# Redrawing the issue order, PSUM banks and exp buffers of a linear-attention + MLP-Mixer kernel

## The chip, the cores and the metric

The kernel runs on one core of a Trainium2 chip. The metric is device microseconds of one execution; the number given is the median of several timed runs. Beside the timed runs stands one execution taken with the hardware profiler, whose trace all views come from.

## What is computed

Linear attention with the ELU+1 feature map over 8 batches, 8 heads, 576 positions and 64 columns a head, then an MLP-Mixer over the 576 x 512 result of each batch: token mixing (576 to 256 and back), and channel mixing (512 to 1536 and back), each with its residual.

```python
def phi(x):
    return np.where(x > 0, x, np.exp(x) - 1.0) + 1.0
q_p, k_p = (phi(q), phi(k))
kv = np.einsum('bhsd,bhse->bhde', k_p, v)
z = np.sum(k_p, axis=2)
num = np.einsum('bhsd,bhde->bhse', q_p, kv)
den = np.einsum('bhsd,bhd->bhs', q_p, z)[..., None] + 1e-06
x = num / den                       # heads side by side: 576 x 512 a batch
...
h = np.maximum(xt @ w_tok1, 0.0) @ w_tok2          # xt: x transposed
u = x + h.transpose(0, 2, 1)
h2 = np.maximum(u @ w_ch1, 0.0) @ w_ch2
return (u + h2).astype(np.float32)
```

## The kernel before

The kernel is a list of 1114 named steps. Each name stands for one short function that issues a handful of instructions on one engine, and a loop at the end (line 1026) walks the string `ORDER` (line 62) and issues the steps as they stand. Every engine and every DMA queue works through its own instructions in that order; waits between engines follow from the data, on whole regions of a buffer: a step waits for every earlier step in the list that touches the same region. Four tables name places: `BANK` the PSUM bank of each accumulator (8 banks), `EBUF` which of three buffers an exponential goes to, `YBUF` and `SLOT` others. All the data of a batch passes through the steps in a pipeline several batches deep, so that at any time four or so batches are in work.

A name begins with its batch (0 to 7; 8 is the set of the last 64 positions of all batches together). Where a step has two halves, a last digit 0 or 1 names it.

- `nLq`, `nLk`, `nLv` (line 223): loads of q, k and v, on SP's queue. `nqT` (330), `nuT` (484) and `nut` (489): DMA transposes of the features of q, of u, and of the tail rows of u, on the same queue.
- `nqx`, `nkx` (ScalarE, 247) the exponential; `nqa`, `nka` (VectorE, 251) max(x + 1, 1); `nqb`, `nkb` (VectorE, 257) the smaller of both. `nv` (270) the cast of v, on ScalarE with two exceptions.
- `nK` (TensorE, 297) the products of k and v of a batch, `nKc` (ScalarE, 303) their two copies out of PSUM; `nn` (TensorE, 383) q times them; `nd` (ScalarE, 393) the denominators, `nnd` (VectorE, 398) the reciprocal, `nn0` to `nn2` and `nnt` (VectorE, 402) and `no` (ScalarE, 423) the scaled results. Batch 1 transposes its q on TensorE (`1Q`, 315) and not by DMA.
- Token mixing: `nf` (TensorE, 450), `nfr` (ScalarE, 455); `ng` (TensorE, 462), `ngu` (VectorE, 468) which adds the residual; `ngt` and `ngv` (475, 479) the same for tail rows of two batches.
- Channel mixing, both products in Strassen-Winograd's form with seven products of blocks. Batch 0 is done plainly (`0m`, `1m` for the first product of batches 0 and 1, line 653, read by `0r`, `1r`, line 660 and 662; `0q`, 674). For the others: `ns1` to `ns4` (VectorE, 790) the sums of blocks of the transposed u; `nxgi` (TensorE, 828) product i of column group g, read by `nygi` (VectorE 648, ScalarE 841 and 843); `nw` (VectorE, 752) sums of blocks of the hidden layer; `npij` (TensorE, 870) product i, half j, of the second product; `nc` (ScalarE, 911) and `neZ`, `neW`, `neY`, `neX` (VectorE, 917) read them, and `nhZ`, `nhW`, `nhY` (GpSimd, 924) add three parts into the output buffer. `ws` (GpSimd, 725) and `G` (VectorE, 802) are sums of weight blocks.
- Output: `noa`, `nob` (GpSimd's queue, 928), `0o0`, `0o1` (685), and for the tails `8R` (VectorE, 883) and `8D` (889).

`nhZ` and `nhY` follow `neZ` and `neY`, `nhW` follows `neW`; X and W share the odd row pairs of the buffer, Z and Y the even ones, and an `nh` waits for whichever `ne` of its rows stands before it in the list.

```python
def pair_more(n, z, i):
    d, c = PAIR[z]
    o = slots(f"{n}P", 4)[:, d::2, HC[c]]
    nc.gpsimd.tensor_tensor(out=o, in0=o, in1=part[i], op=ALU.add)
...
def u_sums(n, which):
    t = tuc
    b11, b12, b21, b22 = [ublock(n, h, e) for h in range(2) for e in range(2)]
    x_, y_ = {1: (b12, b11), 2: (b22, t[0]), 3: (b22, b12), 4: (b21, t[1])}[which]
    (nc.gpsimd if f"{n}s{which}" in ON_POOL else nc.vector).tensor_tensor(
        out=t[which - 1], in0=x_, in1=y_, op=ALU.subtract)
```

Of the kernel before, what the change touches and what calls it, by code (L numbers as in the profile page):

```python
# [41 lines left out]
BANK = {k_: int(v_) for k_, v_ in (e.split(":") for e in """2K:2 2n0:6 2n1:2 2n2:0 2f:5 2g0:4 2g1:1 2X2:4 2Z2:2 2Y2:6 3K:4 3n0:6 3n1:0 3n2:4 3f:0 3g0:0 3g1:0 3X2:6 3Z2:5 3Y2:5  # L42
3gt:7 4K:2 4n0:2 4n1:0 4n2:4 4f:0 4g0:0 4g1:0 4X2:3 4Z2:0 4Y2:2 5K:0 5n0:3 5n1:6 5n2:0 5f:6 5g0:6 5g1:6 5X2:2 5Z2:1
5Y2:0 5gt:5 6K:2 6n0:6 6n1:0 6n2:2 6f:6 6g0:6 6g1:4 6X2:5 6Z2:7 6Y2:4 7K:4 7n0:6 7n1:2 7n2:4 7f:6 7g0:6 7g1:6 7X2:7
7Z2:0 7Y2:3 7gt:0 1h00:1 1h01:3 1h10:2 1h11:4 1t0:5 1t1:1 1t2:3 1t3:0 1m0:4 1m1:2 1m2:5 1m3:1 1m4:3 1m5:6 1m6:0 1m7:5
1m8:1 1m9:5 1m10:4 1m11:5 7X0:0 7Z0:3 7Y0:4 7X1:5 7Z1:6 7Y1:1 1PX:2 1PZ:0 1PY:7 2PX:7 2PZ:6 2PY:6 3PX:2 3PZ:5 3PY:5
4PX:4 4PZ:4 4PY:5 5PX:1 5PZ:2 5PY:0 6PX:2 6PZ:5 6PY:6 warm0:0 0Q00:1 0Q01:2 0s0:3 warm1:0 0Q10:1 0Q11:2 warm2:3 0K0:4
0d0:0 0n0:6 0l0:1 0s1:2 0K1:4 0d1:3 0n1:6 0l1:0 0f0:1 0f1:4 0g00:2 0g01:3 0g10:0 0t0:6 0t1:4 0g11:1 0m0:6 0m1:5 0t2:7
0t3:4 0m2:3 0m3:7 0m4:0 0m5:2 0m6:7 0m7:4 0m8:6 0m9:2 0m10:1 0m11:3 U00:0 U01:5 1Q0:1 U02:6 U03:7 1Q1:1 1K:3 1n00:1
1n01:1 1n10:3 1n11:3 1n20:3 1n21:1 1f:3 2X1:5 2Z1:4 2Y1:7 3X1:3 3Z1:4 3Y1:4 4X1:4 4Z1:1 4Y1:1 5X1:3 5Z1:5 5Y1:7 6X1:3  # L50
6Z1:1 6Y1:6 2X0:3 2Z0:6 2Y0:2 3X0:2 3Z0:4 3Y0:7 4X0:0 4Z0:1 4Y0:5 5X0:6 5Z0:0 5Y0:5 6X0:2 6Z0:0 6Y0:1 1gt:0 7PX:0
7PY:4 7PZ:1 8X0:4 8X1:6 8X2:7 8Y0:2 8Y1:3 8Y2:5 8Z0:1 8Z1:4 8Z2:5 8PX0:7 8PX1:2 8PY0:6 8PY1:3 8PZ0:1 8PZ1:5""".split())}
# [57 lines left out]
def kernel(  # L110
# [134 lines left out]
    def phi_exp(nm, n, c):  # L245
        f = raw[nm, rb(n)][:, 2 * c:2 * c + 2].rearrange("p j f -> p (j f)")
        nc.scalar.activation(out=ebuf[EBUF[f"{n}{nm}{c}"]], in_=f, func=AF.Exp)  # L247

# [808 lines left out]
```

## Time and profile before

| what | value |
|---|---|
| timed runs, us | 249.76, 249.89, 250.34; median 249.89 |
| profiled execution, us | 250.8 |
| its span, first to last instruction, us | 249.0 |
| granted TensorE clock, mean | 0.993 |
| instructions in the trace | 6343 |

The page of the profile gives for each engine the time in which it was busy, its share of the span and its number of instructions; PE is TensorE's matmuls, PEld its weight loads, DVE is VectorE, ACT ScalarE, POOL GpSimd and SP the engine that issues loads and transposes. A list by stretches of time gives the same between two cuts. In a timeline a line has its start, its duration, the engine, the line of code, the operation and its tiles, and in square brackets how long the engine had stood idle and which instruction released it.

### The profile page before, as it was taken

How to read it: one execution, taken by the hardware profiler on the slowest of the kernel's cores; microseconds unless marked ns; L12 is line 12 of the kernel's file. 1: busy time of each engine (PE TensorE's matmuls, PEld its weight loads, DVE VectorE, ACT ScalarE, POOL GpSimd, SP SyncE). 2: the span in 40 equal slices, each digit the busy share in tenths (PEclk: the TensorE clock that was granted, in tenths of full speed). 3: DMA queues.
4: the chain of work that ended last, by engine and by line, in shares of the span. 5: the costliest groups of instructions: out<-in, count | busy, mean ns of one | idle time of the engine just before them, and what ended most of it. 6: DMA issues, size and time to landing. Idle time of an engine off the chain costs nothing.

```text
span 249.0 us, 6343 instructions
## 1 busy us (share of the span) xinstructions
PE 232.2 (93%) x2556; PEld 174.1 (70%) x2570; DVE 218.0 (88%) x374; ACT 147.1 (59%) x268; POOL 81.6 (33%) x93
## 2 busy tenths in 40 slices
...
GB/s 241 263 203 259 343 218 259 406 317 340 307 139 280 371 198 178 364 210 203 194 315 277 69 159 212 327 84 153 113 3 179 99 0 4 5 166 0 8 151 180
DMA packets 50349, 48.55 MB, mean 195 GB/s; under 512 B 30736, under 2 KB 36240, under 8 KB 50320
## 3 DMA queue, kind: packets, MB, share of 16 engines
...
## 4 chain that ended last, share of the span: by engine, by line
PE 71%; DMA 15%; DVE 5%; POOL 3%; issue 2%; ACT 1%; SPq 1%; DVEq 0%; POOLq 0%; ACTq 0%
PE ps L870 26%; PE ps L828 23%; PE ps L450 6%; DMA uT<-u 6%; DMA q_raw<-in_q_dram 5%; DMA wc<-in_moe_w_ch_dram 4%; PE ps L674 4%; PE ps L462 4%; PE ps L653 3%; PE ps L297 2%; PE ps L383 1%; DVE sums L790 1%; POOL qT L966 1%; DVE obuf L917 1%; PE ps L514 1%
## 5 line engine op out<-in xcount | busy, mean ns | idle before, releaser
L828 PEld LDWEIGHTS <-swc 128*128 128x128 bf16 x336 | 32.7, 98 | 7.6 <-DVE sums L790 1.1
L828 PE MATMUL ps<-sums,swc 128*128 128x256 bf16 x252 | 34.4, 273 | 1.2 <-DVE sums L790 1.2
L870 PEld LDWEIGHTS <-cr 128*128 128x128 bf16 x288 | 27.9, 98 | 4.3 <-issue 0.3
L870 PE MATMUL ps<-k_raw,v_raw 128*128 128x256 bf16 x252 | 30.8, 273 | 0.1
L924 POOL TENSOR_TENSOR obuf<-obuf,q_raw 128x512 f32<-128x512 f32 x7 | 9.7, 1381 | 63.5 <-ACT q_raw L911 26.1
L828 PEld LDWEIGHTS <-wc 128*128 128x128 bf16 x252 | 24.5, 98 | 5.0 <-issue 0.8
L843 ACT COPY v_raw<-ps 128x512 f32<-128x512 f32 x35 | 20.3, 593 | 12.1 <-PE ps L828 7.1
L870 PEld LDWEIGHTS <-v_raw 128*128 128x128 bf16 x252 | 24.3, 98 | 3.6 <-issue 0.3
L648 DVE CUSTOM_DVE_ANT_0 cr<-ps,v_raw 128x512 bf16<-128x512 f32 x35 | 23.6, 682 | 2.2 <-PE ps L828 2.1
L928 POOL DMA_DIRECT2D out_dram<-obuf x28 | 17.7, 637 | 23.3 <-DVE obuf L917 16.9
L870 PE MATMUL ps<-wc,cr 128*128 128x256 bf16 x192 | 23.9, 273 | 0.0
L247 ACT ACTIVATE e<-q_raw 128x1152 bf16<-128x1152 f32 x16 | 18.7, 1170 | 8.2 <-DMA q_raw<-in_q_dram 8.0
L917 DVE TENSOR_TENSOR obuf<-ps,u 128x512 f32<-128x512 f32 x28 | 19.2, 686 | 4.7 <-PE ps L870 2.3
L653 PE MATMUL ps<-uT,wc 128*128 128x512 bf16 x92 | 21.5, 379 | 1.6 <-DVE xt L402 1.2
L247 ACT ACTIVATE e<-k_raw 128x1152 bf16<-128x1152 f32 x16 | 18.7, 1174 | 5.6 <-DMA k_raw<-in_k_dram 5.5
L828 PE MATMUL ps<-uT,wc 128*128 128x256 bf16 x144 | 20.6, 272 | 0.3
L841 ACT ACTIVATE cr<-ps 128x512 bf16<-128x512 f32 x21 | 12.0, 599 | 11.1 <-PE ps L828 10.4
L924 POOL TENSOR_TENSOR obuf<-obuf,part 128x512 f32<-128x512 f32 x7 | 9.8, 1406 | 24.5 <-DVE obuf L917 24.4
L653 PEld LDWEIGHTS <-wc 128*128 128x128 bf16 x96 | 9.1, 98 | 11.7 <-issue 1.7
L468 DVE TENSOR_TENSOR u<-ps,x 128x1024 bf16<-128x1024 f32 x12 | 14.6, 1218 | 1.5 <-PE ps L462 1.4
L752 DVE TENSOR_TENSOR v_raw<-cr 128x1536 bf16<-128x1536 bf16 (+3 forms) x21 | 14.1, 683 | 1.6 <-ACT cr L841 1.6
L924 POOL TENSOR_TENSOR obuf<-obuf,w 128x512 f32<-128x512 f32 x7 | 9.0, 1284 | 19.4 <-DVE obuf L917 19.2
...
## 6 DMA issues: line engine op xcount, KB each, us to landing
...
```

The lines of the kernel that those rows point to most:

```text
L247: nc.scalar.activation(out=ebuf[EBUF[f"{n}{nm}{c}"]], in_=f, func=AF.Exp)
L450: nc.tensor.matmul(out=banks(f"{n}f")[:, mt], lhsT=w1t[:, b, ms] if r == R else w1[:, r, ms], rhs=xt[n // 2 % 2] if r == R else x[b][:, r, :],
L468: nc.vector.tensor_tensor(out=u[b][:, rs], in0=banks(f"{n}g{i}"), in1=x[b][:, rs], op=ALU.add)
L648: nc.vector._custom_dve(TENSOR_ADD_SAT, out=o, in0=ps, in1=c, s0=3.4028234663852886e38, s1=0.0)
L653: nc.tensor.matmul(out=bank(f"{n}m{mc}"), lhsT=wc1[:, kj, 128 * mc:128 * mc + 128], rhs=uTj[b][:, kj] if n < 2 - U1 else uT[b][:, :, kj], ...
L752: return engine.tensor_tensor(out=s_[which - 1][:, ks], in0=x_, in1=y_, op=op)
L828: nc.tensor.matmul(out=ps[:, j], lhsT=lhs[:, k_, 128 * j:128 * (j + 1)], rhs=rhs[:, :, k_], start=(first and j == 0 and k_ == 0), stop=(k_ ...
L843: nc.scalar.copy(out={1: c1, 6: c6, 5: c5}[i], in_=ps)
L870: nc.tensor.matmul(out=ps, lhsT=lhs[:, k_], rhs=rhs[:, k_], start=(first and not skip and k_ == 0), stop=(k_ == KH - 1), skip_group_check= ...
L917: nc.vector.tensor_tensor(out=slots(f"{n}P", 4)[:, d::2, HC[c]], in0=pair_tile(n, "X" if z == "W" else z), in1=u[n % 2][:, d::2, HC[c]], o ...
L924: nc.gpsimd.tensor_tensor(out=o, in0=o, in1=part[i], op=ALU.add)
L928: nc.gpsimd.dma_start(out=outv[n, :, 2 * d + e:2 * d + e + 5:4], in_=slots(f"{n}P", 4)[half[e], d::2])
```

## The change

The change replaces three of the tables: `ORDER`, `BANK` and `EBUF`. `ORDER` holds the same 1114 names before and after, in another sequence; the first 56 (to `0mb1`) keep their places. Which engine does a step, the functions behind the names, the loads, buffers and their sizes stay. The sequence of transposes and loads on SP's queue is changed in the middle, and so are the positions of VectorE's steps against the sums on GpSimd. Of the diff, the lines named in the prediction (old ones first):

```diff
--- before.py
+++ after.py
@@ -39,71 +39,71 @@
...
-BANK = {k_: int(v_) for k_, v_ in (e.split(":") for e in """2K:2 2n0:6 2n1:2 2n2:0 2f:5 2g0:4 2g1:1 2X2:4 2Z2:2 2Y2:6 3K:4 3n0:6 3n1:0 3n2:4 3f:0 3g0:0 3g1:0 3X2:6 3Z2:5 3Y2:5
...
+BANK = {k_: int(v_) for k_, v_ in (e.split(":") for e in """2K:2 2n0:2 2n1:0 2n2:4 2f:5 2g0:0 2g1:6 2X2:3 2Z2:0 2Y2:0 3K:2 3n0:2 3n1:6 3n2:0 3f:6 3g0:6 3g1:6 3X2:1 3Z2:3 3Y2:2
...
 
-EBUF = {k_: int(v_) for k_, v_ in (e.split(":") for e in """0k0:0 0q0:1 0q1:2 0k1:0 1k0:1 1k1:0 1q0:0 1q1:1 2q0:2 2q1:1 2k0:0 2k1:2 3q0:1 3q1:0 3k0:1 3k1:2 4q1:2 4q0:2 4k0:1
-4k1:2 5k0:1 5k1:2 5q0:1 5q1:0 6k1:0 6k0:2 6q1:1 6q0:0 7k1:2 7k0:1 7q0:0 7q1:0""".split())}
+EBUF = {k_: int(v_) for k_, v_ in (e.split(":") for e in """0k0:0 0q0:1 0q1:2 0k1:0 1k0:2 1k1:2 1q0:0 1q1:1 2q0:0 2q1:2 2k0:1 2k1:0 3q0:2 3q1:1 3k0:0 3k1:0 4q1:1 4q0:1 4k0:0
+4k1:0 5k0:1 5k1:0 5q0:2 5q1:2 6k1:2 6k0:2 6q1:1 6q0:0 7k1:1 7k0:2 7q0:1 7q1:1""".split())}
 
...
 ORDER = """A2 A0 A1 A3 A4 A5 A6 A8 A9 A7 A10 A12 A13 A14 A11 A16 A17 A15 A19 A18 A21 A20 A22 A23 A24 A25 A26 A27 A28 A29 A30 A33
...
-0ma5 0mb5 0mb3 0ma2 B0 B1 G03 0mb2 0r5 1ka0 G02 G04 1kb0 0ma4 0mb4 0r2 0r4 0mb0 0r0 G21 G11 0r3 G12 0ma10 G22 0mb10
-G14 1kx1 0ma7 0r1 1ka1 0ma9 0mb9 1kb1 B2 2Lq0 0r10 0ma8 0mb8 0r8 0ma6 0mb6 0ma11 G13 0mb7 0r9 0r6 0q0 0mb11 1qx0 1qa0
...
-3qx1 1ma2 1mb2 1r5 2Kc0 2Kc1 1r2 ws20 ws30 1r8 1gv 2n 3qa0 1mb10 2d1 2d0 0o1 2d2 1r10 1ma11 1mb11 1r11 1ma0 1mb0 3qb0
-2nd 2o0 3qa1 2n2 1ma7 2nt 3kx0 1mb7 2o1 1r7 1ma6 1mb6 2n0 1ma3 1mb3 1r6 0o0 2n1 2f0 3qb1 3ka0 2f1 1r0 1r3 1w10 1w13
...
-3y16 2eW 5qa1 5Lv0 2eY 2p41 3y12 5v0 4n1 3x21 2p40 2hW 5Lv1 2eX 3y25 3y21 2hY 5qb1 5qa0 3x02 5qx0 4f1 3s3 4fr1 4f0
-3x26 3x05 4fr0 4g1 3y26 3y02 3y05 5qb0 5ka1 3x15 4gu1 3x23 3y23 3x03 3y06 3x07 2oa 6Lq1 6qx1 2ob 3x17 3y15 5v1 3x27
-4g0 3s4 3y07 3x04 3y27 3x22 3x13 3y17 4gu0 3ut 3y04 5kb1 3x24 3y24 3y22 3x14 3y14 5K 3y13 5Kc1 3p10 3p20 5qT1 3y03
-3w12 6Lv0 5qT0 3p21 3w10 6v0 3p11 3eZ 5Kc0 5n 3w22 5d1 3p50 3p51 5d0 3w20 5d2 3w30 3c0 3w40 5nd 5n2 6Lk1 5n0 3p61 3p60
-3hZ 3c2 3p31 3p30 4uT0 3c1 5o1 3p71 3p70 6ka1 5o0 4x21 6kx1 3eY 6Lk0 6kx0 4uT1 4x11 4s1 4x05 3hY 3oa 4y11 5nt 4x01 3eW
-3hW 6kb1 4y21 3p40 4x12 6Lq0 4s2 4y01 4x06 6ka0 5n1 4y12 6kb0 4x26 6Lv1 3p41 6v1 3eX 6qa0 4s3 6qx0 6qb0 5f0 4x16 6qa1
...
-6y07 7gv 7uT0 6x27 6y16 6x15 6x23 6y27 6y15 6x22 6x17 6y22 6x03 6x24 6y24 6y23 6x04 6x13 7x01 6y04 7x21 6y17 6x14 6y14
...
+0ma8 0ma4 0ma6 1kx0 0mb6 G01 G02 G04 1ka0 1kb0 B0 B1 B2 0ma5 0mb5 G21 G23 0r1 0r0 0r6 2Lq0 2Lq1 2Lv0 G03 0ma11 1kx1
+0mb8 0r8 0mb2 0r2 0mb11 1ka1 1kb1 0r11 G13 0mb4 0r5 0ma7 0mb7 0r4 0ma9 0mb9 G22 0r7 G11 1qx0 0ma10 1qx1 0mb10 G12 0r9
...
+2kx1 1r1 1ma8 1mb8 3qx0 1mb10 2v1 1ma9 2kb0 2ka1 1r8 2kb1 3qx1 1mb4 1r4 1mb5 1r5 0z2 1ma2 1mb2 0z3 1mb9 1r2 1r9 1gt
+1gv 1r10 ws10 2K ws20 1ma3 1mb3 2Kc0 2Kc1 2qT1 3qa0 2qT0 3qb0 2n 1r3 1ma7 1mb7 2d1 3qa1 1ma11 3Lk0 2d0 2d2 2nd 1mb11
+ws32 2n2 2nt 1r7 2n0 2n1 0o1 3Lv1 2o1 2o0 0o0 1r11 1w13 3Lk1 1ma0 1mb0 1r0 ws30 1ma6 1mb6 3qb1 1r6 1w10 2f0 2f1 3ka0
...
+2w30 2w40 3x12 5kx0 5kb0 4n2 2p71 2p70 2c2 2p31 2p30 3x01 5Lk1 5qa1 1ob 3x21 2eW 3y01 2p41 2p40 3y11 2eY 4n1 3y12 2eX
+2hZ 4f1 3s3 2hW 5qb1 5Lv1 4f0 5v1 3y21 6Lk0 3x22 4fr1 3x02 4fr0 4g0 3s1 3x25 5qa0 5qx0 3s2 3y02 4gu0 3x26 3x06 3x15
+5kx1 3y06 4g1 3x16 2hY 5qb0 3y22 3x05 3s4 3y26 3x27 2oa 4gu1 6Lq1 3x07 3y15 3x13 3y25 3y16 5Lv0 3y05 3y27 2ob 3y07
+3x17 3x03 6qx1 5ka1 3y17 3x04 5v0 5kb1 3x24 3y24 3x23 3y23 3x14 3y03 3y04 3y13 6Lv1 3y14 5K 3w10 6v1 5Kc1 3p20 5qT1
+3p10 3p11 5Kc0 3w12 3w20 3w22 5qT0 3c0 5n 5d0 3p21 3w30 4uT1 5d2 3eZ 3p61 5d1 5nd 5o0 5n0 5nt 3p60 3c1 3p50 3p51 3w40
+3c2 3hZ 4uT0 4x02 6Lk1 6ka1 6kx1 3p70 4x12 3p30 5n2 6kb1 4s1 3p31 6kx0 3eY 3hY 3oa 3p71 4x11 3eW 4x21 5n1 4x01 6ka0
+4y11 4s2 3p40 5o1 4y01 3p41 6Lv0 4y02 5f0 6Lq0 6qx0 5f1 4x16 4y12 5fr0 4y21 4x26 3eX 5fr1 5g1 4y16 4x15 4x25 7Lv1 4x06
+4y15 4x05 6kb0 6qa1 7Lq1 4s4 4s3 6qb1 3hW 3ob 4x13 6qa0 4y25 4x23 5gu1 4y26 4x27 4y05 6qb0 4x03 4y27 4y06 4x07 4y07
...
+5p60 4oa 5eZ 7ka1 5c1 5p50 7kb1 7K 7Kc1 5p51 5c2 6gu0 6uT0 5w30 6gu1 6uT1 5p70 5p71 7Kc0 7n 7d0 5w40 5p31 5p30 7d1 5eW
+7d2 5p40 5p41 7nd 7n2 7n1 7o0 7o1 5hW 6x11 6x01 7n0 7nt 5eY 5eX 7f0 7f1 6s1 6s2 6x21 5hZ 7fr0 6y01 6x02 6y11 6s3 7fr1
+6y02 6x12 6y12 6x15 7g0 6x06 6y06 6x05 6y21 6x22 7gu0 6y15 6x16 6y22 6s4 7g1 7gu1 6y05 6x13 6y16 6y13 6x26 6x07 6y07
+6x17 6y17 5hY 6y26 6x03 6x27 6y03 5oa 6x25 6y25 6x04 6x14 6y04 3ut 7gt 6w10 6w20 8x01 7gv 6x23 6y27 6y23 6w30 6p10
+7uT0 7x12 6x24 6y14 6y24 6w12 6w22 6w40 6p11 6c0 6p20 6p21 6p50 6p60 6p61 6c1 6p51 6c2 7x01 6p70 7uT1 7x11 7s1 5ob 7s2
+7s4 7y01 7x06 7x02 7y02 6p71 7y06 7s3 6p31 7y11 6eZ 6hZ 7x15 7y12 7y15 6p30 6eY 7x07 8y01 7x05 7y05 7ut 6hY 7y07 7x21
...
+8R20 8p51 8R51 8w44 7p41 7eX 8w32 8p60 8R60 8p61 8p50 8D210 8R50 8p70 8R70 8p31 8D211 8R61 8R31 8p30 8p71 7hZ 8p40
+8D311 8D310 8R30 8D200 8D201 8R71 8D710 7hY 7oa 8R40 8D711 8D700 8p41 8D701 8R41 8D410 7ob 8D411"""
```

76 lines of the change are left out of this document (33 added, 43 removed).

## The prediction

> **What bounds the kernel now.** I read the busy times first, then their split over seven stretches, cut where the waits of TensorE fall. Columns of a stretch: us from the start, length, busy time (instructions) of PE, PEld, DVE, ACT, POOL, granted clock, DMA share, GB/s.
>
> ```profile
> PE 232.2 (93%) x2556; PEld 174.1 (70%) x2570; DVE 218.0 (88%) x374; ACT 147.1 (59%) x268; POOL 81.6 (33%) x93
> 0.00:34.61 34.61, 29.54 (x264) 16.96 (x267) 26.13 (x56) 20.61 (x40) 16.41 (x28) 1.00 1.06 263
> 34.61:60.11 25.50, 24.92 (x299) 14.28 (x304) 23.96 (x48) 17.15 (x25) 13.98 (x12) 1.00 1.08 305
> 60.11:66.96 6.85, 5.58 (x62) 2.83 (x63) 6.76 (x9) 5.35 (x14) 5.14 (x6) 1.00 0.98 343
> 66.96:122.00 55.04, 54.62 (x700) 42.39 (x702) 53.93 (x85) 41.78 (x73) 13.30 (x14) 1.00 0.90 240
> 122.00:138.00 16.00, 12.94 (x144) 10.63 (x143) 13.91 (x21) 11.23 (x21) 5.47 (x5) 1.00 0.86 261
> 138.00:242.81 104.81, 104.57 (x1093) 86.96 (x1095) 92.84 (x160) 51.00 (x98) 27.29 (x30) 1.00 0.45 103
> 242.81:249.03 6.22, 0.00 (x0) 0.00 (x0) 0.42 (x1) 0.00 (x0) 0.00 (x0) 0.73 0.62 181
> ```
>
> TensorE sets the time, with VectorE close behind: in 66.96 to 122 TensorE idles 0.42 us in 55, VectorE 1.11. So another order can win only what TensorE idles (5.07 before 34.61; 0.58 + 1.27 + 0.42 + 3.06 + 0.24 = 5.57 behind it; 6.22 of final reads and stores), and it loses wherever VectorE, with a few per cent to spare, comes late. The largest piece is 122 to 138. The list of TensorE's waits (total, times, longest) and the timeline (start, duration, engine, operation, count, idle before and its releaser) tell what it is:
>
> ```profile
> PE ps L383 <- ACT kvbd L303: 1.5, 1, 1.5
> PE ps L828 <- DVE sums L790: 1.2, 2, 0.8
> PE ps L653 <- DVE xt L402: 1.2, 1, 1.2
> ...
> 123.50 1.16 ACT L270 CAST vs<-v_raw 128x1152 bf16<-128x1152 f32 x1 [2.23 <-DMA v_raw<-in_v_dram]
> 124.18 7.17 DMA uT<-u
> 124.67 0.38 ACT L303 CAST kvbd<-ps 64x260 bf16<-64x260 f32 x1
> 125.09 0.79 PE L383 MATMUL ps<-kvbd,qT 64*128 64x65 bf16 x40 [1.53 <-ACT kvbd L303]
> 130.90 1.27 POOL L924 TENSOR_TENSOR obuf<-obuf,w 128x512 f32<-128x512 f32 x1 [2.74 <-DVE obuf L917]
> 131.45 1.00 DVE L790 TENSOR_TENSOR sums<-uT 128x512 bf16<-128x512 bf16 x1 [0.70 <-DMA uT<-u]
> 132.50 0.60 PE L828 MATMUL ps<-sums,swc 128*128 128x256 bf16 x4 [0.39 <-DVE sums L790]
> 133.98 1.71 POOL L924 TENSOR_TENSOR obuf<-obuf,part 128x512 f32<-128x512 f32 x1 [0.29 <-DVE obuf L917]
> 134.47 1.50 DVE L790 TENSOR_TENSOR sums<-uT,sums 128x512 bf16<-128x512 bf16 x1
> 136.03 1.05 PE L828 MATMUL ps<-sums,swc 128*128 128x256 bf16 x8 [0.83 <-DVE sums L790]
> ```
>
> ScalarE waits 2.23 us in `6v0` for the load of v, so `5Kc0` behind it is late and `5n` stalls 1.53. Then `4uT1` (the second row of that time, from the chain) lands 7.17 us after its issue, `4s1` and `4s2` wait for it, and each runs long beside a GpSimd sum: 1.00 and 1.50.
>
> ```profile
> L790 DVE TENSOR_TENSOR sums<-uT,sums x6: 414/418/1499, 79.4 to 202.0; 128x512 bf16<-128x512 bf16 x6
> L924 POOL TENSOR_TENSOR obuf<-obuf,part x7: 1264/1285/1711, 80.6 to 238.9; 128x512 f32<-128x512 f32 x7
> L648 DVE CUSTOM_DVE_ANT_0 cr<-ps,v_raw x35: 675/681/693, 83.9 to 227.7; 128x512 bf16<-128x512 f32 x35
> 106.01 0.42 DVE L790 TENSOR_TENSOR sums<-uT,sums 128x512 bf16<-128x512 bf16 x1
> 106.35 0.68 DVE L917 TENSOR_TENSOR obuf<-ps,u 128x512 f32<-128x512 f32 x1
> 106.95 0.75 DVE L251 TENSOR_SCALAR y<-q_raw 128x1152 bf16<-128x1152 f32 x1
> 107.62 0.68 DVE L917 TENSOR_TENSOR obuf<-ps,u 128x512 f32<-128x512 f32 x1
> 107.17 1.66 POOL L924 TENSOR_TENSOR obuf<-obuf,part 128x512 f32<-128x512 f32 x1 [4.97 <-DVE obuf L917]
> ```
>
> The same sum on VectorE takes 414 ns alone (min/median/max of a line) and 1499 beside a GpSimd sum; the GpSimd sum takes 1264 alone and 1711 or 1.66 when an L251 was already running. A read out of PSUM never grows (675 to 693). So the two engines exclude each other where VectorE has SBUF alone as input (L251, L257, L752, L790): the one that comes second waits. The starts also give VectorE's slots: 0.34 for L790, 0.60 for L917 (L648 alike, 0.09 under its 0.68), 0.67 for L251 and L257.
>
> **The change part by part.** The same 1114 steps stand in both lists and each engine runs the same instructions; only orders, banks and E buffers differ. So nothing is costed by the number of instructions, and each place by what TensorE waits there. The slots of TensorE: eight 256-wide matmuls in 1.05 with the last 0.27 (row at 136.03), so 0.11 each; and from the next fence eight 512-wide ones in 1.89 with the last about 0.38, so 0.217.
>
> *Loads and transposes of batches 4 to 6 (122 to 138).* On SP's queue `5qT1 5qT0 4uT1 4uT0` now stand together, behind `6Lv1` and ahead of `6Lk1 6Lv0`; before, loads stood between all four. `6Lv0` moves behind the transposes, and `6v1` takes the place of `6v0` on ScalarE. A pair of transposes without loads between is in the trace:
>
> ```profile
> 72.09 3.03 SPq L484 DMA_TRANSPOSE uT<-u  x2
> ...
> L468 DVE TENSOR_TENSOR u<-ps,x x12: 1210/1218/1225, 70.8 to 191.3; 128x1024 bf16<-128x1024 f32 x12
> ```
>
> Both issued in 3.03 us there, against one that lands after 7.17 here. TensorE's work between `4g0` and the first `4x` that needs the transposes also grows, in slots of the list from 12.4 to 24.1 us (other work, of batches 3 and 5, now stands between), so after the two L468 of 1.2 the pair has over 15 us. The five stalls go: 3.06 of idle, and with each stall the 0.16 by which a 273 ns matmul outlasts its 0.11 slot and which idle time doesn't count: 3.06 + 5 x 0.16 = 3.8. In their place `6v1` (1.16, as at 123.50) runs ahead of both `5Kc` while TensorE has about 2.0 us of work ahead of `5n`: 1.16 + 2 x 0.38 and the hops, 2.2: +0.2. Bounds: −3.8 to 0, if the load under `6v1` is late as `6v0`'s was.
>
> *`2n` to `2f` (60 to 67).* Here stands the 1.2 us wait of TensorE.
>
> ```profile
> 59.52 2.92 POOL L685 DMA_DIRECT2D out_dram<-obuf  x4
> 60.62 1.55 DVE L257 TENSOR_TENSOR qp<-e,y 128x1152 bf16<-128x1152 bf16 x1
> 62.42 1.84 DVE L251 TENSOR_SCALAR y<-q_raw 128x1152 bf16<-128x1152 f32 x1
> 62.46 2.81 POOL L725 TENSOR_TENSOR q_raw<-wc,q_raw 128x512 bf16<-128x512 bf16 x2
> 64.52 0.67 DVE L402 TENSOR_TENSOR xt<-ps,dens 64x512 bf16<-64x512 f32 x1
> 65.24 1.89 PE L653 MATMUL ps<-uT,wc 128*128 128x512 bf16 x8 [1.21 <-DVE xt L402]
> ```
>
> Beside GpSimd's output transfers and weight sums `3qb0` took 1.55 and `3qa1` 1.84 instead of 0.75, and `2nt` came late. The new order puts `3qb0` ahead of `2n`, but also less matmul behind `2n`: 16 + 1 slots of 0.217 = 3.7 against 4.9 before. The chain there is three L393, the reciprocal, L402 and L423: about 4.7. Stall 1.0, 1.8 if output transfers again sit on `3qa1`, against 1.37 with its hidden part: −0.2 (−0.4 to +0.4).
>
> *`7uT0`.*
>
> ```profile
> 189.48 6.82 DMA uT<-u
> ```
>
> It is awaited by `7x01`; with `3ut` and nothing else close ahead of it, it ends sooner: −0.24, all the idle time of that stretch.
>
> *Start.* `1qx0` now follows six L662 on ScalarE instead of three.
>
> ```profile
> 29.72 1.55 ACT L662 ACTIVATE cr<-ps 128x512 bf16<-128x512 f32 x3
> 32.60 1.16 ACT L247 ACTIVATE e<-q_raw 128x1152 bf16<-128x1152 f32 x1 [1.32 <-DMA q_raw<-in_q_dram]
> ```
>
> Six take 3.1 behind a `1kx1` that ends near 29.8: 32.8 against 32.60, +0.2 on the `1Q` that TensorE waits for. Bounds 0 to +0.5.
>
> *GpSimd's sums of batch 2.* The title of the change speaks of clearing products from sums; I checked it step by step. Nothing but its inputs holds a GpSimd sum back, so it starts when the last L917 of its pair ends, wherever it stands in the list. New order of VectorE: `2eW 2eY 4n1 3y12 2eX 3s3 5qb1 3s1 5qa0 3s2 3y02 4gu0 5qb0` and so on. `2hZ` falls on `4n1` and `3y12`, which read PSUM: clear. But `2hW` starts at the end of `2eX` and `2hY` right behind, so `5qb1` and `3s1` (or what stands beside them) each meet a sum of 1.26: 2.5 us late. What is late next is `5kb1`, for which `5K` waits: VectorE has from `2eX` 0.6 + 4 x 0.34 + 5 x 0.67 + 2 x 1.13 + 5 x 0.59 = 10.5 us, TensorE from the end of `2p40` ten and eight 512-wide slots and 17 groups of four 256-wide: 3.9 + 7.4 = 11.3. Of the 0.8 between, hops leave about 0.5: TensorE loses +2.0 (0, if GpSimd comes late or VectorE waited anyway, to +2.5).
> The other batches by the same reading: in batch 3 `3hW` delays `6qa1`, mostly absorbed, +0.1; in 5 `5hZ` and `5hY` delay `6s1`, `6s2`, which only shortens waits for `7g0`, 0; in the tail `7hZ` and `7hY` meet row sums, +0.2; 1, 4 and 6 are clear. Bound if none of it is absorbed: 1.26 + 1.95 + 0.8 = 4.0.
> The Trainium skill (page "SBUF — State Buffer", section "Who interferes with whom") has this as a lock on a shared port pair: two SBUF inputs, or a two-port mode, contend with GpSimd's reads, and whoever issues first holds the pair for the whole instruction. The rows of L790, 414 to 1499, agree. The same section says that an instruction with at most one SBUF input, outside the two-port modes, does not contend; L251 has one, and if that put it out of reach the 0.1 of batch 3 would fall and the sum below would be −1.64. The row of L251 at 62.42, 1.84 beside L725, speaks for contention, so I keep the 0.1.
>
> **Sum.** −3.8 + 0.2 − 0.2 − 0.24 + 0.2 + 2.0 + 0.1 + 0.2 = −1.54, from 249.03 to 247.5. The profiled execution was 250.8 with span 249.03, the median of the timed ones 249.89: I carry 0.86 from span to time, so 248.3. Own range 247.3 to 249.4, from the collision of batch 2 half absorbed (+1.0) to unabsorbed (+0.5 more) with `3qa1` blocked (+0.6 more).
>
> **Rivals.**
> *The sums find room.* `2hW` and `2hY` fall on reads of PSUM, or `5K` has more slack than I see: without the 2.0 and the 0.3, −3.84: span 245.2, 246.1. For: most sums of before ran at 1.26 and cost TensorE nothing (0.42 idle in 55 us). Against: the order above has four SBUF steps in five behind `2eX`.
> *The regrouped queue helps by half.* The load under `6v1` is late as that under `6v0` was, and `5n` stalls its 1.53 + 0.16 as before, in place of the 0.2: −1.54 − 0.2 + 1.69 = −0.05, 249.8 (with `4uT` late too it would be among the slower). For: the DMA share in 122 to 138 is 0.86, and `6v1` comes ahead of `5Kc` on ScalarE. Against: `6Lv1` is issued ahead of the transposes, where `6Lv0` stood among them.
> *Slower: VectorE becomes the bound behind the collisions.* One mechanism: VectorE's SBUF steps in batches 2, 3, 5 and the tail each stand off a whole sum, and none is made up, since VectorE trails TensorE by its slots (53.93 of 55.04 busy). 2.5 + 1.26 + 1.95 + 0.8 = 6.5 against gains of 3.8 + 0.2 + 0.24 − 0.4 = 3.84: +2.7, span 251.7, 252.6. It decides once 3.84 us of VectorE delay reach TensorE. For: 1.11 us to spare in 55. Against: in 138 to 242.81 VectorE has 12 us to spare, and batch 5's collisions and the tail's lie there.
>
> **How the numbers follow.** Forecast 0.42, sums find room 0.22, half the help 0.14, slower 0.22. Two tenths of a per cent, 0.5 us, is what a measurement can tell. Faster: eight tenths of the first and all of the second, 0.56; same: a twentieth of the first and most of the third, whose 249.8 lies inside it: 0.13; slower: the fourth, 0.22, and the rest of the first and the third, 0.31. The range takes most of the second, the whole third and, as the fourth has 252.6 in its middle, some of its milder end: 245.5 to 251.9.
>
> **What would show it.** After: no TensorE wait at `5n` over 0.5 and none on `4s1`, `4s2` (L790 at 414); both `4uT` in under 5 us; an L257 and an L790 of batch 5 and 3 at 1.5 or more right behind `2eX`, and TensorE waiting about 2 us at `5K` (L297) or the steps ahead of it; L402 of batch 2 still awaited for 1. Wrong it would be if SP's waits in order hold a transpose behind a load's buffer, or if a bank given to two close steps makes TensorE wait for a read, which I only checked where the lists place them closer than before.

## The result

| | before | after |
|---|---|---|
| median of the timed runs, us | 250.13 (249.76 to 251.81, 7 runs) | 248.19 (248.05 to 248.69, 7 runs) |
| ratio, with its 95% interval | | 0.9919 (0.9894 to 0.9944) |
| profiled execution, us | 250.8 | 248.69 |
| its span, us | 249.03 | 246.9 |
| TensorE's last matmul ends at | 242.81 | 242.44 |
| from there to the span's end | 6.22 | 4.5 |

The kernel is 1.9 us faster and 248.3 had been forecast. The last two rows already show that the agreement isn't one of reasons: the forecast took nothing from the end of the kernel, and of the 2.1 us by which the span fell, 1.7 lie there.

### The profile after

Two of the stretches, cut as before (us from the start, length, busy time and instructions of PE, PEld, DVE, ACT, POOL, granted clock, DMA share, GB/s), the waits of TensorE that the text uses (total, times, longest), and `4s1` and `4s2` from the timeline:

```profile
66.96:122.00 55.04, 52.22 (x609) 39.72 (x612) 51.45 (x82) 42.23 (x76) 12.51 (x14) 1.00 0.85 252
122.00:138.00 16.00, 15.68 (x231) 12.65 (x230) 15.09 (x25) 11.04 (x22) 4.45 (x5) 1.00 0.72 191
```

```profile
PE ps L450 <- ACT x L423: 1.5, 1, 1.5
...
PE ps L653 <- ACT cr L662: 1.5, 2, 1.2
...
PE ps L828 <- DVE x L402: 0.8, 1, 0.8
PE ps L870 <- DVE v_raw L752: 0.4, 1, 0.4
...
PE ps L383 <- ACT kvbd L303: 0.2, 1, 0.2
```

```profile
133.34 0.42 DVE L790 TENSOR_TENSOR sums<-uT 128x512 bf16<-128x512 bf16 x1
136.40 0.42 DVE L790 TENSOR_TENSOR sums<-uT,sums 128x512 bf16<-128x512 bf16 x1
```

In 122 to 138 TensorE's idle time fell from 3.06 to 0.32: the waits for L790 are gone from the list, and 0.17 is left of the 1.53 for L303. But 66.96 to 122, which had idled 0.42, now idles 2.82, and three waits are new there: L450 for ScalarE's L423, L828 for VectorE's L402, L870 for L752.

Idle time leaves out what a matmul's modelled end covers, so the two traces are compared below by TensorE's loss: the gaps between the starts of neighbouring matmuls, less the median gap behind that line in the kernel before (of two middle gaps the larger), summed over a stretch. It is worked out from the matmuls of each trace; a negative part stands in the first 12 us of both.

| us | before | after | difference | forecast |
|---|---|---|---|---|
| 0 to 40, start | 3.18 | 3.53 | +0.35 | +0.2 |
| 59 to 72, `2n` to `2f` | 2.18 | 3.15 | +0.97 | −0.2 |
| 100 to 118, batch 2's second product | 0.60 | 2.02 | +1.42 | +2.0 |
| 118 to 150, queue of batches 4 to 6, and `3hW` of batch 3 | 5.45 | 2.08 | −3.37 | −3.5 |
| 150 to 230 | 1.22 | 1.48 | +0.26 | −0.24 |
| other stretches of TensorE (the tail in the forecast) | 2.77 | 2.78 | 0 | +0.2 |
| TensorE's end to the span's end | 6.22 | 4.5 | −1.7 | 0 |

The first six add up to −0.37, TensorE's end, and the whole to −2.1, the span. A row is good to some 0.2 to 0.3 us. Some matmuls have no record (L653 shows 92 matmuls and 96 weight loads), and a gap that spans one counts as loss. And the gaps behind L475 alternate between 3 and 236 to 312 ns, so that its groups of four matmuls count too little. One such group lies across 150 before the change and wholly ahead of it after; with the mean gap of each line over the matmuls that wait for nothing, the rows are +1.03 for 59 to 72, −3.14 for 118 to 150 and −0.03 for 150 to 230.

### The profile page after: what moved, and what is told of

Same layout as the page of the kernel before. It is cut to its first block, busy times and chain, and to the rows that moved or that the text cites. A ratio compares the mean times of both kernels' runs of the same rounds, so it can differ in the third digit from the quotient of the medians.

```text
span 246.9 us, 6333 instructions
## 1 busy us (share of the span) xinstructions
PE 233.2 (94%) x2556; PEld 173.4 (70%) x2570; DVE 216.1 (88%) x374; ACT 146.1 (59%) x268; POOL 79.0 (32%) x93
## 4 chain that ended last, share of the span: by engine, by line
PE 65%; DVE 6%; ACT 2%; issue 1%; DVEq 0%; ACTq 0%
PE ps L870 26%; PE ps L828 26%; PE ps L450 5%; PE ps L462 4%; DVE x L402 2%; PE ps L297 1%; PE ps L383 1%; ACT x L423 1%; DVE v_raw L752 1%; PE ps L475 1%; DVE y L251 1%; DVE xt L402 1%; DVE obuf L917 1%; ACT vs L270 0%; DVE dens L398 0%
## 5 line engine op out<-in xcount | busy, mean ns | idle before, releaser
L828 PEld LDWEIGHTS <-swc 128*128 128x128 bf16 x336 | 32.9, 98 | 5.7
L828 PE MATMUL ps<-sums,swc 128*128 128x256 bf16 x252 | 32.7, 273 | 0.0
L870 PE MATMUL ps<-k_raw,v_raw 128*128 128x256 bf16 x252 | 31.1, 273 | 0.4 <-DVE v_raw L752 0.4
L870 PEld LDWEIGHTS <-cr 128*128 128x128 bf16 x288 | 27.8, 98 | 4.1
L843 ACT COPY v_raw<-ps 128x512 f32<-128x512 f32 x35 | 19.8, 595 | 17.3 <-PE ps L828 12.1
L828 PEld LDWEIGHTS <-wc 128*128 128x128 bf16 x252 | 24.4, 98 | 5.7 <-issue 1.9
L924 POOL TENSOR_TENSOR obuf<-obuf,q_raw 128x512 f32<-128x512 f32 x7 | 9.4, 1341 | 57.2 <-DVE obuf L917 31.7
L870 PEld LDWEIGHTS <-v_raw 128*128 128x128 bf16 x252 | 24.2, 98 | 4.5 <-DVE v_raw L752 0.9
L870 PE MATMUL ps<-wc,cr 128*128 128x256 bf16 x192 | 24.3, 273 | 0.0
L653 PE MATMUL ps<-uT,wc 128*128 128x512 bf16 x92 | 22.0, 379 | 2.0 <-ACT cr L662 1.5
L928 POOL DMA_DIRECT2D out_dram<-obuf x28 | 17.7, 638 | 9.9 <-DVE obuf L917 7.8
L924 POOL TENSOR_TENSOR obuf<-obuf,part 128x512 f32<-128x512 f32 x7 | 8.9, 1273 | 36.9 <-DVE obuf L917 36.9
L828 PE MATMUL ps<-uT,wc 128*128 128x256 bf16 x144 | 19.3, 272 | 1.1 <-DVE x L402 0.8
L653 PEld LDWEIGHTS <-wc 128*128 128x128 bf16 x96 | 9.1, 97 | 12.5 <-issue 2.3
L924 POOL TENSOR_TENSOR obuf<-obuf,w 128x512 f32<-128x512 f32 x7 | 8.9, 1270 | 23.9 <-DVE obuf L917 23.8
L752 DVE TENSOR_TENSOR v_raw<-cr 128x1536 bf16<-128x1536 bf16 (+3 forms) x21 | 14.0, 684 | 2.8 <-ACT cr L662 1.5
L450 PE MATMUL ps<-x,w 128*128 128x512 bf16 x50 | 14.2, 379 | 1.8 <-ACT x L423 1.5
```

The source lines that it names most:

```text
L450: nc.tensor.matmul(out=banks(f"{n}f")[:, mt], lhsT=w1t[:, b, ms] if r == R else w1[:, r, ms], rhs=xt[n // 2 % 2] if r == R else x[b][:, r, :],
L653: nc.tensor.matmul(out=bank(f"{n}m{mc}"), lhsT=wc1[:, kj, 128 * mc:128 * mc + 128], rhs=uTj[b][:, kj] if n < 2 - U1 else uT[b][:, :, kj], ...
L752: return engine.tensor_tensor(out=s_[which - 1][:, ks], in0=x_, in1=y_, op=op)
L828: nc.tensor.matmul(out=ps[:, j], lhsT=lhs[:, k_, 128 * j:128 * (j + 1)], rhs=rhs[:, :, k_], start=(first and j == 0 and k_ == 0), stop=(k_ ...
L843: nc.scalar.copy(out={1: c1, 6: c6, 5: c5}[i], in_=ps)
L870: nc.tensor.matmul(out=ps, lhsT=lhs[:, k_], rhs=rhs[:, k_], start=(first and not skip and k_ == 0), stop=(k_ == KH - 1), skip_group_check= ...
```

## The experiments

All times are medians, with the ratio to the kernel before and its 95% interval; the kernel before, run beside them, was between 249.8 and 250.6, so kernels of different experiments are compared by these ratios (0.9919 for the changed kernel). The span is that of the one profiled execution, and lies 1.8 us below the time of that execution.

### Batch 4's scaled rows: a wait of VectorE for a step of ScalarE

Timeline of the changed kernel around the new wait at 105 (start, duration, engine, operation, idle before and its releaser):

```profile
101.86 0.63 DVE L917 TENSOR_TENSOR obuf<-ps,u 128x512 f32<-128x512 f32 x1
102.98 0.59 ACT L911 COPY w<-ps 128x512 f32<-128x512 f32 x1 [0.48 <-PE ps L870]
103.46 0.53 ACT L423 ACTIVATE x<-ps,dens 128x64 bf16<-128x64 f32 x2
104.02 0.96 DVE L402 TENSOR_TENSOR x<-ps,dens 128x768 bf16<-128x768 f32 x1 [1.53 <-ACT x L423]
```

VectorE was through with `2eZ` at 102.49 and stood still until 104.02: `4n0` (L402) writes x, which `4o0` (L423) ahead of it in the list also writes, and `4o0` stood on ScalarE behind `2c1` (L911), which waited for TensorE's product. The edit of the list:

```diff
-... 4o1 2p61 2eZ 2p50 2p51 2c1 4o0 4n0 ...
+... 4o1 4o0 2p61 2eZ 2p50 2p51 2c1 4n0 ...
```

> The changed kernel with the step 4o0 (ScalarE, L423) listed right behind 4o1 instead of behind 2c1. Theory: VectorE's 4n0 idled 1.53 us because it writes the same rows of x as 4o0, which stood on ScalarE behind 2c1, a copy that waits for TensorE; this alone made TensorE wait 0.78 at L828 (3x11) and 0.42 at L870 (2p71). Then both waits go and the time falls by about 1.4 us, from 248.2 to 246.8. Rival: VectorE is behind anyway at this place (its own work, or GpSimd's sum 2hZ), then 4n0 starts earlier but the waits only move and the time stays within 0.4 us of 248.2.

247.48 us, ratio to the kernel before 0.9873 (0.9827 to 0.9920), span 245.5. `4n0` starts at 102.79 behind 0.45 us of idle time instead of 1.53, TensorE no longer waits at L828, waits 0.28 instead of 0.42 at L870, and its loss from 100 to 118 falls from 2.02 to 0.94. TensorE's end comes 1.4 us earlier (241.06); 0.3 of that lies ahead of 100, where nothing was changed, so the edit is worth about 1.1. By the ratios it is 1.1 as well, with intervals that overlap; the trace is the better witness. The first theory holds in its mechanism, with a gain smaller than its 1.4.

### Batch 2's scaled rows: `3qa1` beside output transfers

```diff
-... 2d1 3qa1 1ma11 3Lk0 2d0 2d2 2nd 1mb11 ws32 2n2 2nt 1r7 2n0 2n1 0o1 3Lv1 2o1 2o0 ...
+... 2d1 1ma11 3Lk0 2d0 2d2 2nd 2o1 2o0 1mb11 ws32 2n2 2nt 1r7 2n0 2n1 3qa1 0o1 3Lv1 ...
```

> The changed kernel with 2o1 and 2o0 listed right behind the reciprocal 2nd, and VectorE's 3qa1 behind 2n1 instead of ahead of 2nd. Theory: the 1.51 us wait of 2f0 on 2o0 comes from 3qa1, which took 1.62 beside GpSimd's output transfers and sums and held the reciprocal back by 0.9, and from 2o1 and 2o0 waiting for 2n1. Then 3qa1 meets no transfer, the wait at 2f0 falls below 0.3 and the time by about 1.4 us, to 246.8. Rival: the delay of 3qa1 is passed on to 3qb1 and 3K behind it, then a wait appears at L297 or L828 of batch 3 and the time stays within 0.4 us of 248.2.

246.56 us, 0.9833 (0.9788 to 0.9878), span 244.8. The same steps in the changed kernel, and then in this one:

```profile
60.81 2.68 POOL L685 DMA_DIRECT2D out_dram<-obuf  x4
62.45 1.62 DVE L251 TENSOR_SCALAR y<-q_raw 128x1152 bf16<-128x1152 f32 x1
63.99 0.40 DVE L398 RECIPROCAL dens<-dens 128x42 f32<-128x42 f32 x1
67.33 0.93 ACT L423 ACTIVATE x<-ps,dens 128x64 bf16<-128x64 f32 x4 [3.15 <-DVE x L402]
68.31 0.81 PE L450 MATMUL ps<-x,w 128*128 128x512 bf16 x3 [1.51 <-ACT x L423]
```

```profile
62.88 0.42 DVE L398 RECIPROCAL dens<-dens 128x42 f32<-128x42 f32 x1 [0.64 <-ACT dens L393]
63.34 0.93 ACT L423 ACTIVATE x<-ps,dens 128x64 bf16<-128x64 f32 x4 [0.48 <-DVE dens L398]
64.80 1.89 PE L653 MATMUL ps<-uT,wc 128*128 128x512 bf16 x8 [0.79 <-ACT cr L662]
66.07 0.74 DVE L251 TENSOR_SCALAR y<-q_raw 128x1152 bf16<-128x1152 f32 x1
```

The reciprocal comes 1.1 us earlier and L423 4 us earlier; `2f0` waits no more. Part comes back as 0.79 at `1ma0`, since L662 now stands behind L423. The loss from 59 to 72 falls from 3.15 to 1.55. Which share of it is due to `3qa1` and which to the place of L423 wasn't tried apart; in the changed kernel `3qa1` held the reciprocal for some 0.9 us, and L423 then stood 2.9 us behind the reciprocal, until the last L402 ahead of it in the list was done.

### Loads between the transposes

```diff
 order of SP's queue
-... 5qT1 5qT0 4uT1 4uT0 6Lk1 6Lv0 6Lq0 ...
+... 5qT1 6Lv0 5qT0 6Lk1 4uT1 6Lq0 4uT0 ...
```

> The changed kernel with loads put back between the four transposes on SP's queue: 5qT1, load, 5qT0, load, 4uT1, load, 4uT0, as before the change. Theory of the grouped queue: the transposes land late again (6 us and more for one of uT), 4s1 and 4s2 are late and TensorE waits 1.5 to 3 us between 122 and 138; the time is 249.7 to 251. Rival, the cover: what removed the waits is that TensorE's work between 4g0 and the first 4x grew from 12 to 24 us; then the transposes may land 2 to 4 us later and nothing waits, and the time stays within 0.4 us of 248.2.

253.87 us, 1.0154 (1.0073 to 1.0234), span 251.0. The span is 4.1 longer than in the changed kernel, TensorE's loss from 118 to 134.5 grows by 4.16 (1.45 to 5.61), and the time is worse than either theory had. SP's queue in the changed kernel, and in this one with its longest waits of TensorE:

```profile
117.35 2.76 SPq L330 DMA_TRANSPOSE qT<-qp  x2
120.20 2.96 SPq L484 DMA_TRANSPOSE uT<-u  x2
```

```profile
117.34 1.49 SPq L330 DMA_TRANSPOSE qT<-qp  x1
121.85 0.37 SPq L223 DMA_DIRECT2D v_raw<-in_v_dram  x1
122.27 1.56 SPq L330 DMA_TRANSPOSE qT<-qp  x1
...
127.22 2.39 SPq L484 DMA_TRANSPOSE uT<-u  x1
```

```profile
PE ps L828 <- DMA uT<-u: 2.8, 1, 2.8
PE ps L383 <- DMA qT<-qp: 1.8, 1, 1.8
```

`6Lv0` waits until 121.85 for its buffer, which `5v0` reads to 121.82, and the transposes behind it on the queue wait with it; the last is issued at 127.22 instead of about 121.7. The cover, the 24 us of other work on TensorE between `4g0` and the first `4x`, did not hold; but the last transpose is issued 5.5 us later, and the theory of cover spoke of 2 to 4, so this shows that the cover is not enough here; what it is worth by itself stays open. The next run takes a load that waits for nothing:

```diff
 order of SP's queue
-... 5qT1 5qT0 4uT1 4uT0 6Lk1 6Lv0 6Lq0 ...
+... 5qT1 6Lq0 5qT0 4uT1 4uT0 6Lk1 6Lv0 ...
```

> The changed kernel with one load, 6Lq0, between 5qT1 and 5qT0; its buffer has been free since 115.3, so it waits for nothing. It tells apart why loads between transposes cost 4 us in the run with all of them put back. Theory of the blocked queue: only 6Lv0, which waited till 121.85 for its buffer, held the transposes up; then one free load delays 5qT0 by its issue, 0.5, and TensorE by less than 0.3: 248.2 to 248.5. Rival, shared bandwidth: the 576 KB are moved ahead of the three transposes behind them, which land 1.5 to 2 us later; 5n waits 1.5 more and the time is about 249.7.

249.31 us, 0.9973 (0.9942 to 1.0004), span 247.0. It lies between the two theories: `5n` waits 0.79 instead of 0.17, the loss from 118 to 134.5 is 2.07 instead of 1.45. By the DMA view between 115 and 133 (time from issue to landing last) the two qT took 5.5 us instead of 3.9 and the uT 5.2 instead of 4.8:

```profile
qT<-qp SPq DMA_TRANSPOSE x2, 5.5
uT<-u SPq DMA_TRANSPOSE x2, 5.2
```

So one free load costs 0.6 us of loss in the profiled execution, and 1.4 by the ratios of the times. In the run with three loads about 3 of the 5.5 us by which the last transpose is issued later are the wait of `6Lv0` for its buffer, and the rest is the issuing of the loads; these weren't put back one by one.

### The two halves on the kernel before

Grouping alone, on the order before:

```diff
 order of SP's queue; 6v0 moves behind 6v1 on ScalarE
-... 5qT1 6Lv0 5qT0 6Lk1 4uT0 6Lk0 4uT1 6Lq0 6Lv1 ...
+... 5qT1 5qT0 4uT0 4uT1 6Lk1 6Lk0 6Lv0 6Lq0 6Lv1 ...
```

> The kernel before, with 5qT1 5qT0 4uT0 4uT1 together on SP's queue and the loads 6Lk1, 6Lk0 and 6Lv0 behind them (6v0 moves behind 6v1 on ScalarE); TensorE's order, and with it the cover of 12 us, stays. Theory of the queue: the transposes land within 5 us, 4uT1 some 5 us earlier, the five waits between 122 and 138 shrink from 3.8 to less than 1 us: time about 247. Rival, cover: the waits on 4s1 and 4s2 stay since VectorE and GpSimd meet there anyway (1.00 and 1.50 for L790), and only the wait of 5n goes: about 248.3.

250.50 us, 1.0015 (0.9993 to 1.0036): no gain. The transposes no longer hold anything, `5n` doesn't wait, and yet the loss from 118 to 150 only falls from 5.45 to 4.48. The timeline shows what is left:

```profile
126.34 1.33 POOL L924 TENSOR_TENSOR obuf<-obuf,q_raw 128x512 f32<-128x512 f32 x1 [12.36 <-ACT q_raw L911]
126.46 2.03 DVE L752 TENSOR_TENSOR q_raw<-cr,v_raw 128x1536 bf16<-128x1536 bf16 x1
128.54 1.48 PE L870 MATMUL ps<-wc,q_raw 128*128 128x256 bf16 x12 [0.48 <-DVE q_raw L752]
133.23 1.23 POOL L928 DMA_DIRECT2D out_dram<-obuf  x2 [0.30 <-POOL obuf L924]
133.84 2.22 DVE L790 TENSOR_TENSOR sums<-uT,sums 128x512 bf16<-128x512 bf16 x1
134.48 1.28 POOL L924 TENSOR_TENSOR obuf<-obuf,part 128x512 f32<-128x512 f32 x1
136.11 1.05 PE L828 MATMUL ps<-sums,swc 128*128 128x256 bf16 x8 [1.55 <-DVE sums L790]
```

`3w40` (L752) stands off GpSimd's `3hZ`, `4s2` (L790) first the issue of two output transfers (L928, to 134.46) and then `3hW`, and TensorE waits for both. In the changed order the two sums of GpSimd run beside reads of PSUM. That was tried on the order before as well, with a wait for each sum, which also stands behind the step it waits for in the list:

```diff
-        nc.gpsimd.tensor_tensor(out=o, in0=o, in1=part[i], op=ALU.add)
+        after(nc.gpsimd.tensor_tensor(out=o, in0=o, in1=part[i], op=ALU.add),
+              live[{"Z": "5nd", "W": "6ka0"}[z]] if n == 3 and z in "ZW" else None)
```

> The kernel before with the transposes grouped as in the run of the grouped queue, and two of GpSimd's sums made to wait for a step of VectorE: 3hZ for 5nd and 3hW for 6ka0, so that 3hZ runs beside 5n2 and 5n0 and 3hW beside 5n1 and 4y12, which read PSUM. Grouping alone left TensorE a loss of 3.85 us between 120 and 140 (4.74 before, 1.71 after the change), with 3w40 at 2.03 and 4s2 at 2.21 us. Theory: what was left are these two collisions; then 3w40 is 0.95, 4s2 0.42, the loss falls to about 1.7, and the time by 2 us against the grouped queue, to 248.3. Rival: TensorE then waits for something else of the old order in the same place (its cover is only 12 us, 5nd and 6ka0 come late themselves), the loss stays above 3 and the time at 250.

249.80 us, 0.9998 (0.9958 to 1.0039), span 247.5. The collisions are gone:

```profile
125.19 0.95 DVE L752 TENSOR_TENSOR q_raw<-cr,v_raw 128x1536 bf16<-128x1536 bf16 x1
126.61 1.26 POOL L924 TENSOR_TENSOR obuf<-obuf,q_raw 128x512 f32<-128x512 f32 x1 [13.89 <-DVE dens L398]
131.49 0.42 DVE L790 TENSOR_TENSOR sums<-uT,sums 128x512 bf16<-128x512 bf16 x1
133.75 2.21 ACT L270 CAST vs<-v_raw 128x1152 bf16<-128x1152 f32 x2 [1.73 <-DMA v_raw<-in_v_dram]
140.07 0.81 PE L462 MATMUL ps<-ar,w2p 128*128 128x512 bf16 x3 [1.16 <-ACT ar L455]
```

The loss up to 134.5 is 1.09, but 2.92 from there to 150: the casts `6v1` and `6v0`, which this experiment had put together ahead of `6qx0`, wait 1.73 for loads that are now behind the transposes, and ScalarE is late for `5fr1`. The last run moves the casts:

```diff
-... 6Lv1 3p41 6v1 6v0 3eX ... 5fr1 5g1 ... 4y16 4x15 ...
+... 6Lv1 3p41 3eX ... 5fr1 6v1 5g1 ... 4y16 6v0 4x15 ...
```

> The kernel before with the transposes grouped and the two sums cleared as in the run before, and ScalarE's casts 6v1 and 6v0 moved from ahead of 6qx0 to behind 5fr1 and 4y16. In that run TensorE's loss from 118 to 134.5 us was 1.09 (3.60 before), but 2.92 from 134.5 to 150 (1.85 before, 0.63 after the change), with ScalarE waiting 1.73 us in the casts for the loads behind the transposes. Theory: the regrouped queue, the cleared sums and casts that don't wait are together what the change did in this stretch; then both losses are 1.0 to 1.5 and 0.6 to 1.0, and TensorE's loss over the stretch about 2 us, as in the changed kernel, for a span near 246.5. Rival: something else of the new order is needed too, and the loss from 134.5 to 150 stays above 2.

248.00 us, 0.9942 (0.9914 to 0.9971), span 246.2. The losses are 0.91 and 1.03, in all 1.94 against 5.45 before and 2.08 after the change. With these three edits in one place and nothing else of the new order, the kernel before loses in this stretch no more than the changed one. Its time comes out near that of the changed kernel (0.9942 against 0.9919, the intervals overlap) for another balance: it keeps its long end (6.1 us) and has none of the two new waits. Transposes that stand together, sums that run beside reads of PSUM and casts that stand behind their loads' landing are enough together. Grouping alone, and grouping with the sums cleared, gained no time; the sums or the casts without the grouping weren't tried.

### The collision that the prediction priced

```diff
-        nc.gpsimd.tensor_tensor(out=o, in0=o, in1=part[i], op=ALU.add)
+        after(nc.gpsimd.tensor_tensor(out=o, in0=o, in1=part[i], op=ALU.add),
+              live["e", 2, "X"] if (n, z) == (2, "W") else None)
```

> The changed kernel with one wait added: GpSimd's 2hW waits for VectorE's 2eX, which the prediction took for granted. Theory of the prediction's price: 2hW and 2hY then run beside 3s3, 5qb1 and 3s1, these stand off 1.26 us each, VectorE is 2.5 us later and TensorE loses about 2.0 at 5K or ahead of it: 250.2. Rival: VectorE has more room here than the prediction's 0.5 us (it waited 1.5 us for 4o0 shortly before, and TensorE with it), L257 and L790 grow to 1.5 or more but TensorE loses less than 0.5 us: 248.2 to 248.7.

250.05 us, 0.9978 (0.9951 to 1.0004), span 247.9. With the wait put in, the collision comes as it was described:

```profile
111.87 1.33 POOL L924 TENSOR_TENSOR obuf<-obuf,part 128x512 f32<-128x512 f32 x1 [8.46 <-ACT q_raw L843]
112.00 1.81 DVE L257 TENSOR_TENSOR qp<-e,y 128x1152 bf16<-128x1152 bf16 x1
113.16 1.78 POOL L924 TENSOR_TENSOR obuf<-obuf,w 128x512 f32<-128x512 f32 x1
113.73 1.49 DVE L790 TENSOR_TENSOR sums<-uT 128x512 bf16<-128x512 bf16 x1
115.27 0.60 PE L828 MATMUL ps<-sums,swc 128*128 128x256 bf16 x4 [0.40 <-DVE sums L790]
```

Two steps of VectorE lose 1.07 and 1.08 (1.81 against 0.74, 1.49 against 0.41). TensorE's loss from 100 to 134.5 grows from 3.46 to 4.92, by 1.46, and first of all where `3x25` waits for `3s1`, not at `5K`. In the changed kernel itself `2eW` and `2eY` (the first row), `2hW` and `2eX` (the last) stand so:

```profile
108.90 1.27 DVE L917 TENSOR_TENSOR obuf<-ps,u 128x512 f32<-128x512 f32 x2
109.70 1.27 POOL L924 TENSOR_TENSOR obuf<-obuf,part 128x512 f32<-128x512 f32 x1 [5.81 <-DVE obuf L917]
111.56 0.67 DVE L917 TENSOR_TENSOR obuf<-ps,u 128x512 f32<-128x512 f32 x1
```

`2hW` started at 109.70, right after its own `2eW`, ahead of `2eX` which stands before it in the list, and ran beside `4n1` and `3y12`. So an `nh` waits for its own `ne` alone, and not, as the section on the kernel before has it, for whichever `ne` of its rows stands before it: X and W share rows, but `PAIR` gives them other columns.

### The stores at the end

The output transfers `7ob` of GpSimd's queue made to wait for a late read of VectorE (`8R71`):

```diff
-            nc.gpsimd.dma_start(out=outv[n, :, 2 * d + e:2 * d + e + 5:4],
-                                in_=slots(f"{n}P", 4)[half[e], d::2])
+            after(nc.gpsimd.dma_start(out=outv[n, :, 2 * d + e:2 * d + e + 5:4],
+                                      in_=slots(f"{n}P", 4)[half[e], d::2]),
+                  live["R", 7, 1] if (n, d) == (7, 1) else None)
```

> The changed kernel with one wait added: the output transfers 7ob of GpSimd's queue wait for the read 8R71 of VectorE, so that they are issued about 2.0 us ahead of TensorE's end, as before the change, and not 4.9 ahead. Theory: the 1.7 us that the last stores took longer before (242.8 to 249.0 against 242.4 to 246.9) come from 7ob's transfers being issued among them; then the stretch from TensorE's end to the span's end grows from 4.5 to about 6, the issues of L889 on SP and ScalarE take 1 to 1.9 us again, and the time is about 249.7. Rival: the stores of L889 are faster for their own order (two on each queue closer together), and 7ob plays no part; then the stretch stays 4.5 to 4.8 and the time 248.2.

251.11 us, 1.0029 (0.9999 to 1.0059), span 249.9. First the kernel before, then the changed one, then this one:

```profile
240.80 1.23 POOL L928 DMA_DIRECT2D out_dram<-obuf  x2 [0.66 <-DVE kp L883]
243.13 1.88 ACTq L889 DMA_DIRECT2D out_dram<-kp  x1
```

```profile
236.34 2.43 POOL L928 DMA_DIRECT2D out_dram<-obuf  x4 [0.30 <-POOL obuf L924]
242.64 0.58 ACTq L889 DMA_DIRECT2D out_dram<-kp  x1
243.31 0.55 ACTq L889 DMA_DIRECT2D out_dram<-qp  x1
```

```profile
241.92 1.20 POOL L928 DMA_DIRECT2D out_dram<-obuf  x2 [4.28 <-DVE qp L883]
242.69 0.57 ACTq L889 DMA_DIRECT2D out_dram<-kp  x1
243.36 1.59 ACTq L889 DMA_DIRECT2D out_dram<-qp  x1
```

TensorE ends at 242.50, as in the changed kernel, and the stretch behind it grows from 4.5 to 7.4 us. Before the change the last two L928 went out 2.0 us ahead of TensorE's end and a store of L889 behind them took 1.88 to issue; after it all four were out by 238.8, and the issues take 0.55. The wait came 1.4 us later than meant, so it also overshoots. The other way round, on the kernel before:

```diff
-... 7eW 7hW 8p50 8p60 8R60 8p31 8p61 8D211 8R61 8R31 7p41 8R50 8p70 8R70 7p40 8D311 7eX ...
+... 7eW 7hW 8p50 8p60 8R60 7p41 7p40 7eX 8p31 8p61 8D211 8R61 8R31 8R50 8p70 8R70 8D311 ...
```

> The kernel before, with 7p41, 7p40 and 7eX listed behind 8R60 and so 7ob issued some 2 us earlier than 240.8; nothing else changes. Theory of the late store: the stretch behind TensorE's end falls from 6.2 to about 4.5 us and the time from 249.9 to about 248.3. Rival: the stores of L889 set it by their own order and stay as they are: 249.9.

250.07 us, 0.9999 (0.9971 to 1.0028), span 247.8. The stretch behind TensorE's end is 4.5 instead of 6.2, as the theory has it, but `7p41` now waits 0.60 for `7eW` and `8p30` 0.65, TensorE loses 1.6 us more, and the time stays, so the forecast of 248.3 failed. The cause of the end is shown from both sides; the gain needs products that are there early without a wait.

### Both kernels beaten

The edits of the first two experiments, and at the start:

```diff
-... G03 0ma11 1kx1 0mb8 0r8 0mb2 0r2 0mb11 1ka1 ...
+... G03 0ma11 0mb8 0r8 0mb2 0r2 1kx1 0mb11 1ka1 ...
```

> The changed kernel with three edits of the order: 4o0 ahead of 2c1; 2o1 and 2o0 behind 2nd with 3qa1 behind 2n1; and at the start the exponential 1kx1 behind the reads 0r8 and 0r2 on ScalarE, which wait for nothing while it waits for its load. The first two alone gave spans of 245.5 and 244.8 against 246.9. If they add up: 246.9 - 1.4 - 2.1 = 243.4, and the start gives 0.3 to 0.5 of the 1.23 that 0ma9 waits (the rest goes into the wait for 1qx0's load): span about 243.0, time about 244.4. Rival: batch 4's fix is worth less where batch 2's has moved TensorE ahead of VectorE, the sum is about 1 us less: span 244.0, time 245.4.

244.92 us, 0.9799 (0.9741 to 0.9856), span 243.0: by the ratios 3.0 us less than the changed kernel. The span is that of the theory, in which the edits add up; the median time lies between it and the rival. `0ma9`, which waited 1.23 in the changed kernel, waits for nothing, and `1Q01` takes over a part: it waits 1.31 instead of 0.62 for `1qx0`'s chain, and ScalarE comes to `1qx0` straight from its L662, without waiting for the load.

## Why the prediction was right, point by point

The number was right and the largest term was near in size; three other terms were wrong, and it is luck that they cancel. In differences the forecast was −1.54; the medians differ by 1.94 and the two profiled spans by 2.1.

- **Queue and transposes, −3.6: near in size (−3.4, or −3.1 with the mean gaps), half right in cause.** The waits at `5n`, `4s1` and `4s2` went as the prediction said; L790 is back at 0.42. But it credited the transposes with all of it, though it had read that `4s1` and `4s2` ran long beside GpSimd's sums. On the order before, grouping alone took 1.0 off the loss; the other 2.5 came with `3hZ` and `3hW` cleared of `3w40` and `4s2` and with the casts `6v0` and `6v1` behind the landing of their loads. The cover of 24 us, on which the prediction leaned, did not save the run with loads between. The 3.03 us that the prediction set against a landing of 7.17 is a time of issue; that earlier pair landed in 3.1, so the reading stands.
- **`2n` to `2f`, −0.2: wrong, +1.0.** The step that failed is the stall of 1.0, in which `3qa1` meets no transfer. `3qa1` stood in front of the reciprocal, took 1.62 beside GpSimd's transfers and held it for some 0.9, so `2o0` ended 5.7 us behind `2n` and not "about 4.7"; without those 0.9 the chain is as long as the prediction had it. TensorE waits 1.51 at `2f0` and 0.29 at `1ma0`, 1.8 together, which is the stall that the prediction gave for this collision and put into its upper bound (+0.4). What makes up the rest of the +1.0 wasn't taken apart.
- **Batch 2, +2.0: +1.4, for another reason.** The step that failed is "`2hW` starts at the end of `2eX`": the sum doesn't wait for `2eX`, which writes other columns, and so the collision isn't there (`2hZ`, too, had run at 102.63 behind `2eZ`). By the run that forces it, it would have cost 1.46, not 2.0. The 1.4 that was lost is the wait of `4n0` for `4o0` behind `2c1`, which the prediction passed over, though it names L423's part in the same chain of batch 2. That the size is near is luck. The rival in which the sums find room had the right reading of this place: `2hW` and `2hY` fell on reads of PSUM.
- **Start, +0.2: +0.35**, but the kernels that share the changed start had 2.25 to 3.54 there, so nothing can be said of 0.2.
- **`7uT0`, −0.24: it went**, and a wait of the same size at `6x11` came.
- **Batch 3 and the tail, +0.3: nothing was seen of it.** `3hW` ran from 137.32 beside reads of PSUM, and TensorE loses 0.04 behind 230 in both kernels.
- **End: the largest omission.** The prediction counted the 6.22 us as "final reads and stores" and left them fixed. They fell by 1.7, since the issue of the last output transfers of batch 7 began 4.9 us ahead of TensorE's end and not 2.0.

The lock that the Trainium skill states (page "SBUF — State Buffer", section "Who interferes with whom") is seen in three more places here: L752 at 2.03 against 0.95, L257 at 1.81 against 0.74, and L924 at 1.78 against 1.26 where VectorE was first. The L924 of 1711 ns that the prediction set beside an L251 stood behind an L257 (133.81 to 134.56), which changes nothing in its reading.
